# Second forward attention: wo products of kv heads 0 to 2 between the softmax steps of the last group

## The chip, the cores and the metric

The kernel runs on one core of a Trainium2 chip, in one launch. The metric is the time on the device in microseconds (us); the kernel before is given as the median of three runs.

## The reference

The program computes a small decode network and all its gradients. The forward pass is two layers, each an attention block A and a feed-forward block B, with the same weights in both:

```python
x = A_x                                        # (2, 1, 1024)
x = x + _A_ref(_layernorm(x), A_k_cache, A_v_cache, A_wq, A_wo)
x = x + _B_ref(_layernorm(x), B_w1, B_b1, B_w2, B_b2)
x = x + _A_ref(_layernorm(x), A_k_cache, A_v_cache, A_wq, A_wo)
x = x + _B_ref(_layernorm(x), B_w1, B_b1, B_w2, B_b2)
```

`_A_ref` makes 32 query heads of 128 from `x @ wq`, 8 for each of 4 kv heads, scores them against a K cache of 16384 rows for each batch and kv head, takes the softmax, multiplies with the V cache, and returns `o @ wo` with `wo` of 4096 x 1024. `_B_ref` normalises once more and is `gelu(y @ w1 + b1) @ w2 + b2` with F = 3584. The outputs are the result and the gradients for x, both caches, wq, wo, w1, b1, w2 and b2, from a given `grad_out`. Everything is bf16 outside the chip.

## The kernel before

**Stages.** The order in time is: attention forward of layer 0, feed-forward of layer 0, attention forward of layer 1, feed-forward of layer 1, then the backward passes in the reverse order, with the cache gradients of both layers written at the end. The program is written out in order by hand: each engine executes its instructions in the order in which the kernel issues them, and only semaphores stand between engines.

**Groups and steps.** A group is one of 8 pairs of batch and kv head (g = batch x 4 + kv head). `attn_fwd` (L561) walks over 8 groups x 4 chunks x 4 blocks = 128 slots, one per step: eight 128 x 128 blocks of K are transposed on PE (`emit_T`, L480), copied out of PSUM, and two steps later multiplied with q (`score`, L633). Other work is hung on later steps: `Sched.later(n, f)` runs `f` at the start of the step `n` further on, and `Sched.q` is a queue from which a step takes one entry after that (in every second step while there are slots, in each step afterwards). The walk goes on past the last slot until both are empty.

After a group's last score, `post` (L572) lays out its softmax: the maximum (`p1` and `p2`, 2 and 4 steps on), sixteen exponentials on ACT in pairs (`ex`, 5 to 12 steps on, the first eight for chunks 0 and 1), the products with V (`queue_acc`, four entries 9 steps on and four more, with the closing `fin`, 13 steps on), the sum of the exponentials (14 and 15 steps on). `fin` copies the accumulator out (`evac`, L516), and two steps later `reduce` (L524) folds it on PE and `finish` (L609) writes the group's column of `oT` on DVE. The accumulator is one PSUM tile `ACCT` of 128 x 512 (`acc_all` in the profile); even groups use its left half, odd groups the right.

**The wo product.** When the walk has ended, `attn_layer_fwd` (L805) copies `oT` into `o_all` (L817) and calls `w_fwd` (L341), which clears the left half of `ACCT` (L345) and goes over wo in 8 tiles of 512 rows, 1 MB each. `w_take` (L328, DMA at L331) takes a buffer and issues the load on SP's queue; `fwd_rows` (L334, matmul at L337) makes the 32 products of a tile, 128 x 128 weights against 128 x 32 columns, accumulating in PSUM. Tile k holds the rows of query heads 4k to 4k + 3, so tiles 0 to 5 belong to kv heads 0 to 2, and tiles 6 and 7 to kv head 3, whose second batch is the last group. Then `xA` (L820) adds the residual, two layer norms follow, and w1's 7 tiles and their products (`m_all`), `hpre` (L830), the gelu, and, since layer 1 is the last, the backward pass with w1's and wo's tiles (`weights_down`, L876).

**Buffers.** All streamed tiles (K, V and weights) share one pool `ld` of 7 buffers of 1 MB. A load on SP's queue waits until the last reader of its buffer is done, and whatever SP has to issue next waits behind it. The K and V tiles of group 7 (`keepK`, `keepV`) are loaded in layer 0 and stay in SBUF: `kv_load` (L464) issues nothing for them in layer 1.

Of the kernel before, what the change touches and what calls it, by code (L numbers as in the profile page):

```python
# [23 lines left out]
def kernel(  # L24
# [25 lines left out]
    V = nc.vector  # L50
# [3 lines left out]
    B, _, D = A_x.shape  # L54
    _, HKV, SK, DH = A_k_cache.shape
    assert B == 2 and DH == 128
    HQ = A_wq.shape[1] // DH
# [3 lines left out]
    DJ = D // 128  # L61
    FJ = F // 128
    HD = HQ * DH
    G = B * HKV
    T = SK // 128
    TC = 32
    NCH = T // TC
# [8 lines left out]
    WIDE = 32  # L76
# [56 lines left out]
    ACCT = pa([128, 512], F32, "acc_all")  # L133
# [177 lines left out]
    def w_tiles(W, n_in, n_out):  # L311

        out = []
        if n_out == 1024:
            for j0 in range(0, n_in // 128, 4):
                out.append((j0, 4, 0, 1024))
        elif n_out < 4096:
            for c0 in range(0, n_out, 1024):
                cw = min(1024, n_out - c0)
                nj = 4096 // cw  # L320
                for j0 in range(0, n_in // 128, nj):
                    out.append((j0, nj, c0, cw))
        else:
            for j0 in range(n_in // 128):
                out.append((j0, 1, 0, n_out))
        return out

    def w_take(W, j0, nj, c0, cw):  # L328
        wt = ld.tile([128, LDW], BF16, name="wt", tag="ld")
        wv = wt[:].rearrange("p (j n) -> p j n", j=nj)  # L330
        nc.sync.dma_start(wv, W[j0 * 128:(j0 + nj) * 128, c0:c0 + cw].rearrange("(j p) n -> p j n", p=128))  # L331
        return wv
# [8 lines left out]
    def w_fwd(W, n_in, n_out, x, between=None):  # L341
        JO = n_out // 128
        nw = min(WIDE, 512 // JO)
        fps = ACCT[:, 0:JO * nw].rearrange("p (j b) -> p j b", b=nw)
        V.memset(fps, 0.0)  # L345
        for j0, nj, c0, cw in w_tiles(W, n_in, n_out):
            fwd_rows(fps, nw, w_take(W, j0, nj, c0, cw), x, j0, c0 // 128)
            if between:
                between.popleft()()
        while between:  # L350
            between.popleft()()
        return fps[:, :, 0:2]
# [111 lines left out]
    def kv_load(w, g, c):  # L464
        keep = w + str(c) if g == G - 1 else w if (g, c) == (XG, 0) else None
        t = held_tiles[keep] if keep else ld.tile([128, LDW], BF16, name="kv_" + w, tag="ld")
        if keep not in held:
            src = Kv if w == "K" else Vv
            nc.sync.dma_start(t[:].rearrange("p (t d) -> p t d", d=128), src[g, :, c * TC:(c + 1) * TC, :])
            if keep:  # L470
                held.add(keep)
        return t[:].rearrange("p (t d) -> p t d", d=128)
# [85 lines left out]
                sc_.later(2, a.reduce)  # L558
            sc_.q.append(fin)

    def attn_fwd(l, q_bf, rbc, oT, groups):  # L561
        sch = Sched()
        slots = [(g, c, b) for g in groups for c in range(NCH) for b in range(NB)]
        kTs, sc, st = {}, {}, {}

        def max_half(g, f):
            m = small.tile([128, 8], F32, name="mx%d" % f)
            V.tensor_reduce(out=m[:], in_=sc[g][f][:], axis=AX.X, op=ALU.max)
            charge("D", 0.7)
            st[g].append(m)  # L570

        def post(g):  # L572
            max_half(g, 1)
            m0, m1 = st[g]
            V.tensor_tensor(out=m0[:], in0=m0[:], in1=m1[:], op=ALU.max)
            esum = small.tile([128, 2, 8], F32, name="esum")
            negm = small.tile([128, 8], F32, name="negm")
            box = {}

            def p1():  # L580
                box["pm"] = pm_([8, 128], F32, "pm")
                PE.transpose(box["pm"][:, :], m0[:], identf[:])
                gm = small.tile([8, 1], F32, name="gm")
                V.reduce_max(out=gm[:], in_=box["pm"][:, :], axis=AX.X)
                box["dg"] = small.tile([8, 8], F32, name="dg")
                V.tensor_scalar(out=box["dg"][:], in0=identf[0:8, 0:8], scalar1=gm[:, 0:1], scalar2=None, op0=ALU.mult)
                charge("D", 0.5)

            def p2():
                pm2 = pm_([128, 8], F32, "pm2")  # L590
                PE.matmul(pm2[:], lhsT=onesf[0:8, :], rhs=box["dg"][:], start=True, stop=True)
                V.tensor_scalar(out=negm[:], in0=pm2[:], scalar1=-1.0, scalar2=None, op0=ALU.mult)  # L592
                charge("D", 0.2)

            def ex(f, h):
                half = NP // 2
                S.activation(out=e_all[:, g, f * half:(f + 1) * half, l, h, :],  # L597
                             in_=sc[g][f][:, h, :].rearrange("p (a b) -> p a b", b=2),
                             func=ACT.Exp, bias=negm[:, h:h + 1], scale=1.0, accum_out=esum[:, f, h:h + 1])
                charge("A", 0.3)  # L600

            def fin1():
                V.tensor_tensor(out=esum[:, 0, :], in0=esum[:, 0, :], in1=esum[:, 1, :], op=ALU.add)

            def fin2():
                pm3 = part_sum(esum[:, 0, :], 8, "pm3")
                V.reciprocal(out=rbc[:, g, :], in_=pm3[:])

            def finish(ps):  # L609
                V.tensor_tensor(out=oT[:, g, :], in0=ps, in1=rbc[:, g, :], op=ALU.mult)  # L610

            a = Acc(g, "V", lambda u: e_all[:, g, u, l].rearrange("p h t -> p (h t)"), finish, g % 2)
            sch.later(2, p1)
            sch.later(4, p2)
            for i in range(16):
                sch.later(5 + i // 2, lambda i=i: ex(i // 8, i % 8))
            sch.later(9, lambda: queue_acc(sch, a, range(0, 2), False))
            sch.later(13, lambda: queue_acc(sch, a, range(2, 4), True))
            sch.later(14, fin1)
            sch.later(15, fin2)  # L620

        def score(s):
            g, c, b = slots[s]
            if c == 0 and b == 0:
                sc[g] = {}
                st[g] = []
            kT = kTs.pop(s)
            for j in range(8):
                t = c * TC + b * 8 + j
                f = t // TH  # L630
                if t % TH == 0:
                    sc[g][f] = px([128, 8, TH], F32, "sc")
                PE.matmul(sc[g][f][:, :, t % TH], lhsT=kT[:, j, :], rhs=q_bf[:, g, :], start=True, stop=True)  # L633
            if c == NCH // 2 - 1 and b == NB - 1:
                max_half(g, 0)
            if c == NCH - 1 and b == NB - 1:
                post(g)

        cv = None
        s = 0  # L640
        while s < len(slots) + 2 or sch.busy():
            sch.s = s
            if s < len(slots):
                g, c, b = slots[s]
                if b == 0:
                    cv = kv_load("K", g, c)
                kTs[s] = emit_T(cv, b, True)
            sch.run_slot(1 if s < len(slots) else 2)
            if 2 <= s < len(slots) + 2:
                score(s - 2)  # L650
            s += 1
# [138 lines left out]
    o_all = cols4(HQ, "o_all")  # L790
# [9 lines left out]
    ALLG = list(range(G))  # L800

    def lsl(l):
        return slice(2 * l, 2 * l + 2)

    def attn_layer_fwd(l, xT, between=None):  # L805
        y, rstd = ln_fwd(xT[:], f"a{l}")
        V.tensor_copy(out=n_all[:, 0:DJ, lsl(l)], in_=y[:])
        qps = w_fwd(A_wq, D, HD, n_all[:, 0:DJ, lsl(l)], between)
        qT_bf = vec.tile([128, G, 8], BF16, name=f"qT_bf{l}")
        for b in range(2):  # L810
            V.tensor_scalar(out=qT_bf[:, b * HKV:(b + 1) * HKV, :].rearrange("p k r -> p (k r)"), in0=qps[:, :, b],
                            scalar1=QSCALE, scalar2=None, op0=ALU.mult)
        rbc = vec.tile([128, G, 8], F32, name=f"rbc{l}")
        oT = vec.tile([128, G, 8], F32, name=f"oT{l}")
        attn_fwd(l, qT_bf, rbc, oT, ALLG)
        for b in range(2):
            V.tensor_copy(out=o_all[:, 0:HQ, 2 * l + b], in_=oT[:, b * HKV:(b + 1) * HKV, :].rearrange("p k r -> p (k r)"))  # L817
        aps = w_fwd(A_wo, HD, D, o_all[:, 0:HQ, lsl(l)])
        xn = vec.tile([128, DJ, 2], F32, name=f"xA{l}")
        V.tensor_tensor(out=xn[:], in0=aps, in1=xT[:], op=ALU.add)  # L820
        saved[f"a{l}"] = dict(y=y, rstd=rstd, qT_bf=qT_bf, rbc=rbc, oT=oT)
        return xn
# [559 lines left out]
    sch = Sched()  # L1382
# [128 lines left out]
    while 2 * m < NS + 2:  # L1511
# [7 lines left out]
        for k in range(2):  # L1519
            s = 2 * m + k  # L1520
            if s < NS:
                i, b = NCH + s // NB, s % NB
# [97 lines left out]
```

## Time and profile before

| what | value |
|---|---|
| three runs | 1137.77, 1140.46, 1141.27 us |
| median | 1140.46 us |
| the profiled execution: its own time | 1139.88 us |
| its span | 1138.1 us |
| mean granted PE clock | 0.857 of full speed |
| busy share of the span: PE, DVE, ACT, POOL | 80%, 54%, 47%, 6% |
| DMA, mean over the span | 395 GB/s, 449.2 MB |

The span is the profiled execution from its first to its last instruction, and all places in the text, such as "at 418 us", are measured from the span's start. Busy shares are averages over stages with different limits, so a stage is read in its own window. PE is the matmul engine and PEld its weight loads, DVE the vector engine, ACT the scalar engine, POOL the general one, and SP only issues DMAs. L-numbers are lines of the kernel before.

### The profile page before, as it was taken

How to read it: one execution, taken by the hardware profiler on the slowest of the kernel's cores; microseconds unless marked ns; L12 is line 12 of the kernel's file. 1: busy time of each engine (PE TensorE's matmuls, PEld its weight loads, DVE VectorE, ACT ScalarE, POOL GpSimd, SP SyncE). 2: the span in 40 equal slices, each digit the busy share in tenths (PEclk: the TensorE clock that was granted, in tenths of full speed). 3: DMA queues.
4: the chain of work that ended last, by engine and by line, in shares of the span. 5: the costliest groups of instructions: out<-in, count | busy, mean ns of one | idle time of the engine just before them, and what ended most of it. 6: DMA issues, size and time to landing. Idle time of an engine off the chain costs nothing.

```text
span 1138.1 us, 38123 instructions
## 1 busy us (share of the span) xinstructions
PE 915.9 (80%) x16766; PEld 674.7 (59%) x16767; DVE 619.8 (54%) x1363; ACT 534.0 (47%) x1356; POOL 70.2 (6%) x124
## 2 busy tenths in 40 slices
PE   4979795468888975789887678888898897899996
PEld 3867674358766754778765567755545454455552
DVE  1545451180545523654442246678798767786876
ACT  0544351005544420434333214468697766676764
POOL 0000000000000000000000000022121111111210
PEclk9988895567999875899998678999999978897978
DMA  8999999999999979999999699998999999999997
GB/s 371 423 425 425 424 424 413 395 413 423 423 425 423 412 288 404 388 422 421 399 413 393 232 380 309 370 386 302 403 419 421 421 419 424 423 411 421 423 385 290
DMA packets 104183, 449.20 MB, mean 395 GB/s; under 512 B 7238, under 2 KB 11334, under 8 KB 66896
## 3 DMA queue, kind: packets, MB, share of 16 engines
q1 hardware_dynamic: 86672, 354.46, 77.6%
q0 software_dynamic: 17344, 92.29, 19.6%
q8 instruction: 131, 2.15, 0.7%
q14 instruction: 36, 0.29, 0.1%
HBM read 348.14 MB, written 98.58 MB: 393 GB/s over the span
## 4 chain that ended last, share of the span: by engine, by line
PE 45%; DMA 35%; DVE 10%; issue 5%; ACT 4%; POOL 0%; SPq 0%; DVEq 0%; ACTq 0%; POOLq 0%
DMA kv_V<-in_A_v_cache_dram 13%; PE tp L480 10%; DMA wt<-in_B_w_dram 5%; PE acc_all L512 4%; PE tpm L1527 4%; DMA kv_K<-in_A_k_cache_dram 4%; PE xm L1336 4%; DMA wt<-in_A_wo_dram 3%; DMA out_dram<-keepK 3%; DMA keepK<-in_A_v_cache_dram 3%; PE sc L633 3%; PE xm L1250 2%; PE wtp L358 2%; PE dp L1389 2%; PE dp L726 2%
## 5 line engine op out<-in xcount | busy, mean ns | idle before, releaser
L159 ACT COPY kT<-tp 128x512 int32<-128x512 int32 x200 | 117.4, 587 | 298.4 <-PE tp L480 289.1
L162 DVE COPY kT<-tp 128x1024 bf16<-128x1024 bf16 x168 | 114.9, 690 | 141.8 <-PE tp L480 130.4
L480 PE MATMUL tp<-ident,kv_K 128*128 128x128 bf16 x1728 | 142.0, 230 | 6.9 <-DMA kv_K<-in_A_k_cache_dram 6.8
L480 PEld LDWEIGHTS <-kv_K 128*128 128x128 bf16 x1728 | 107.8, 103 | 7.7 <-DMA kv_K<-in_A_k_cache_dram 7.5
L170 DVE CAST big<-xm 128x512 bf16<-128x512 f32 x133 | 86.3, 684 | 19.3 <-PE xm L1336 14.3
L167 ACT CAST big<-xm 128x512 bf16<-128x512 f32 x151 | 82.1, 595 | 25.0 <-PE xm L1336 14.8
L633 PE MATMUL sc<-qT_bf,kT 128*128 128x8 bf16 x2048 | 91.5, 171 | 0.1
L633 PEld LDWEIGHTS <-kT 128*128 128x128 bf16 x2048 | 75.7, 97 | 26.7 <-issue 20.8
L337 PEld LDWEIGHTS <-wt 128*128 128x128 bf16 x1920 | 57.4, 104 | 54.7 <-issue 17.8
L167 ACT CAST keepV<-xm 128x512 bf16<-128x512 f32 (+1 forms) x137 | 75.0, 594 | 29.5 <-PE xm L1336 18.5
L480 PE MATMUL tp<-ident,kv_V 128*128 128x128 bf16 x864 | 70.2, 227 | 14.1 <-DMA kv_V<-in_A_v_cache_dram 12.2
L597 ACT ACTIVATE e_all<-sc,negm 128x64 bf16<-128x64 f32 x256 | 77.2, 343 | 1.0 <-DVE negm L592 1.0
L170 DVE CAST keepV<-xm 128x512 bf16<-128x512 f32 (+1 forms) x101 | 65.9, 684 | 18.9 <-PE xm L1336 12.7
L269 DVE STREAM_TRANSPOSE wt<-wt 128x512 int32<-128x512 int32 x104 | 63.6, 674 | 14.2 <-PE w2b_f L337 11.0
L512 PE MATMUL acc_all<-kv_V,e_all 128*16 128x256 bf16 x864 | 46.0, 293 | 28.7 <-DMA kv_V<-in_A_v_cache_dram 14.4
L159 ACT COPY wt<-wtp 128x512 int32<-128x512 int32 x72 | 40.3, 587 | 57.0 <-PE wtp L358 54.1
L480 PEld LDWEIGHTS <-kv_V 128*128 128x128 bf16 x864 | 55.2, 101 | 16.2 <-DMA kv_V<-in_A_v_cache_dram 13.1
L597 ACT ACTIVATION_READ_ACCUMULATOR e_all<-sc,negm 128x1 f32 x256 | 59.8, 234 | 0.0
L167 ACT CAST keepK<-xm 128x512 bf16<-128x512 f32 x98 | 53.0, 596 | 14.1 <-PE xm L1336 7.5
L1389 PE MATMUL dp<-wdo,kT 128*128 128x64 bf16 x896 | 52.8, 206 | 0.0
L358 PE MATMUL wtp<-ident,wt 128*128 128x128 bf16 x576 | 47.8, 244 | 4.9 <-ACT wt L159 2.6
L1336 PE MATMUL xm<-QmK,blk 64*128 64x512 bf16 x256 | 48.8, 444 | 2.3 <-ACT keepV L167 1.0
(387 smaller groups left out, 1564.4 us busy)
## 6 DMA issues: line engine op xcount, KB each, us to landing
kv_K<-in_A_k_cache_dram SPq DMA_DIRECT2D x81, 1024.0 KB, 13.0
kv_V<-in_A_v_cache_dram SPq DMA_DIRECT2D x81, 1024.0 KB, 12.9
wt<-in_B_w_dram SPq DMA_DIRECT2D x42, 1024.0 KB, 12.9
wt<-in_A_wo_dram SPq DMA_DIRECT2D x32, 1024.0 KB, 9.6
out_dram<-big POOLq DMA_DIRECT2D x26, 1024.0 KB, 18.9
out_dram<-keepV POOLq DMA_DIRECT2D x19, 1024.0 KB, 20.7
out_dram<-keepK POOLq DMA_DIRECT2D x17, 1024.0 KB, 17.8
wt<-in_A_wq_dram SPq DMA_DIRECT2D x16, 1024.0 KB, 11.0
```

Of the source, the lines that this page charges most:

```text
L159: S.copy(out=dst.bitcast(I32), in_=src.bitcast(I32))
L162: V.tensor_copy(out=dst, in_=src)
L167: S.copy(out=dst, in_=src)
L170: V.tensor_copy(out=dst, in_=src)
L269: V.transpose(out=w, in_=w)
L358: PE.transpose(tp[:, o, :], view[:, o * 128:(o + 1) * 128], ident[:])
L480: PE.transpose(tp[:, j, :], cv[:, b * 8 + j, :], ident[:])
L512: PE.matmul(self.acc[cg:cg + 16, :], lhsT=coef(u), rhs=self.cv[:, t:t + 2, :].rearrange("p t d -> p (t d)"), start=False, stop=True, tile_ ...
L597: S.activation(out=e_all[:, g, f * half:(f + 1) * half, l, h, :], in_=sc[g][f][:, h, :].rearrange("p (a b) -> p a b", b=2), func=ACT.Exp, ...
L633: PE.matmul(sc[g][f][:, :, t % TH], lhsT=kT[:, j, :], rhs=q_bf[:, g, :], start=True, stop=True)
L1336: PE.matmul(pss[k][:], lhsT=blk[p:p + 64, o + 2 * h + k // 2, :], rhs=Qm[p:p + 64, :, :].rearrange("p a b -> p (a b)"), start=True, stop=T ...
L1389: PE.matmul(dp[:, :, t:t + 4], lhsT=kT[:, j, :], rhs=wd[:, :, x:x + 4], start=(b + j == 0), stop=False)
```

## The change

In layer 1 the products of wo's tiles 0 to 5 are issued inside the walk of `attn_fwd`, after group 6 has finished; tiles 6 and 7 follow after it, as before. For that the left half of `ACCT` is cleared, and the part of `o_all` for kv heads 0 to 2 copied, one step after group 6's `finish`; the products of the six tiles are hung 2, 3, 8, 13, 15 and 15 steps after it. The copy for kv head 3 comes after the walk. In layer 0 all eight tiles come after the walk, with the clear ahead of the copy. `w_fwd` is no longer called for wo.

```diff
-    def attn_fwd(l, q_bf, rbc, oT, groups):
+    def attn_fwd(l, q_bf, rbc, oT, groups, early=None):
...
             def finish(ps):
                 V.tensor_tensor(out=oT[:, g, :], in0=ps, in1=rbc[:, g, :], op=ALU.mult)
+                if early and g == groups[-2]:
+                    for at, f in zip((1, 2, 3, 8, 13, 15, 15), early):
+                        sch.later(at, f)
...
-        attn_fwd(l, qT_bf, rbc, oT, ALLG)
-        for b in range(2):
-            V.tensor_copy(out=o_all[:, 0:HQ, 2 * l + b], in_=oT[:, b * HKV:(b + 1) * HKV, :].rearrange("p k r -> p (k r)"))
-        aps = w_fwd(A_wo, HD, D, o_all[:, 0:HQ, lsl(l)])
+        tiles = w_tiles(A_wo, HD, D)
+        heads = HQ // HKV * (HKV - 1)
+        n_early = heads // 4 if l == 1 else 0
+        x = o_all[:, 0:HQ, lsl(l)]
+        fps = ACCT[:, 0:DJ * WIDE].rearrange("p (j b) -> p j b", b=WIDE)
+        wv = {}
+
+        def o_in(k0, k1):
+            n = HQ // HKV
+            for b in range(2):
+                V.tensor_copy(out=o_all[:, k0 * n:k1 * n, 2 * l + b],
+                              in_=oT[:, b * HKV + k0:b * HKV + k1, :].rearrange("p k r -> p (k r)"))
+
+        def take(k):
+            wv[k] = w_take(A_wo, *tiles[k])
+
+        def open_early():
+            V.memset(fps, 0.0)
+            o_in(0, HKV - 1)
+            for c in range(NCH):
+                kv_load("V", G - 1, c)
+            for k in range(n_early):
+                take(k)
+
+        def rows(k):
+            fwd_rows(fps, WIDE, wv.pop(k), x, 4 * k, 0)
+
+        attn_fwd(l, qT_bf, rbc, oT, ALLG, [open_early] + [lambda k=k: rows(k) for k in range(n_early)] if n_early else None)
+        if not n_early:
+            V.memset(fps, 0.0)
+        o_in(HKV - 1 if n_early else 0, HKV)
+        for k in range(n_early, len(tiles)):
+            take(k)
+            rows(k)
+        aps = fps[:, :, 0:2]
```

## The prediction

> **What bounds the kernel now.** I read the page first, for the 40 slices. One slice is 28.45 us, so slice 15 is 398 to 427 us. The third line is what all DMA queues moved.
>
> ```profile
> DMA  8999999999999979999999699998999999999997
> GB/s 371 423 425 425 424 424 413 395 413 423 423 425 423 412 288 404 388 422 421 399 413 393 232 380 309 370 386 302 403 419 421 421 419 424 423 411 421 423 385 290
> ```
>
> The kernel lives on DMA: most slices stand at 410 to 425 GB/s. Slice 15, the end of the second forward attention, is the first deep hole, at 288. The windows around it place it: us, busy time and count of PE, PEld, DVE, ACT, POOL, then the granted clock, the DMA share and GB/s.
>
> ```profile
> 414.00:420.00 6.00, 4.58 (x77) 3.30 (x78) 1.48 (x7) 0.02 (x1) 0.00 (x0) 0.50 0.24 91
> 420.00:424.00 4.00, 4.00 (x157) 4.00 (x154) 0.00 (x0) 0.00 (x0) 0.00 (x0) 0.51 0.68 182
> 424.00:445.00 21.00, 10.16 (x274) 9.25 (x269) 3.53 (x17) 0.00 (x0) 2.11 (x5) 0.58 1.06 403
> ```
>
> From 414 to 424 the queue moved 6 x 91 + 4 x 182 = 1274 KB where 403 GB/s would have moved 4030: 2756 KB short, or 6.8 us of transfer time. Who holds it back is in the waits of SP's queue between 408 and 424 us (total, times, longest):
>
> ```profile
> SPq L331 <- PE acc_all L337: 13.7, 5, 11.3
> ```
>
> SP stood 11.3 us in one wait of `w_take` for a wo product: the load of wo's eighth tile needs the buffer of the first, of seven, and the first is read only after the last group's softmax. Last the chain of waits, 408 to 448 us (start, length), for what the hole costs:
>
> ```profile
> 409.18 4.86 ACT e_all L597 x32
> 414.03 0.04 issue
> 414.08 1.03 PE acc_all L512 x12
> ...
> 416.65 0.43 DVE acc_sb L170
> ...
> 418.96 1.03 PE acc_all L337 x32
> 420.00 0.02 issue
> 420.01 6.93 DMA wt<-in_A_wo_dram
> 426.95 0.04 issue
> 426.99 1.02 PE acc_all L337 x32
> ...
> 431.58 13.38 DMA wt<-in_B_w_dram
> ...
> 447.89 15.19 DMA wt<-in_B_w_dram
> ```
>
> Exponentials, value products, the copy of the accumulator and (left out) the reduction, the first wo products; then 6.93 us waiting for a tile that could only be asked for at 420.01; and from there two waits on w1 tiles (forward, landing 444.96; backward, landing 463.08). The DMA stream is unbroken from about 424 to 478 us, so these landings move with the moment at which the stream restarts.
>
> **What moves.** In the built program the order on SP, ACT and POOL is unchanged: six of wo's loads stood ahead on SP anyway, and the extra call for the last group's V tiles issues nothing, since those tiles stay in SBUF from the first layer. The matmuls are the same; wo groups of 32 stand elsewhere. Counting steps: the last group's `post` runs in step 129, group 6 finishes in 134, so the clear and the copy stand in 135, groups 0 and 1 in 136 and 137 (ahead of all value products, which begin in 138), group 2 in 142 (ahead of the second half), group 3 in 147 (behind the accumulator copy, ahead of the reduction), groups 4 and 5 in 149, behind it. Prices are in PE's order of time (start, length):
>
> ```profile
> 411.71 1.88 PE L512 MATMUL acc_all<-keepV,e_all 128*16 128x256 bf16 x32 [1.82 <-ACT e_all L597]
> 418.96 5.39 PE L337 MATMUL acc_all<-o_all,wt 128*128 128x32 bf16 x197 [0.82 <-DVE acc_all L345]
> ```
>
> 5.39 / 197 x 32 = 0.88 us for a group of 32. Five w1 groups, from 436.36, took 4.41 there, 0.88 each too.
>
> **Costs, step by step.** (1) DVE: group 6's `oT` stands at 409.93 in DVE's order of time. From `oT` to the first product, through two copies and the clear, took 418.19 to 418.96 = 0.77 us, so group 0 starts at 410.70. DVE idles there (3.96 us until L603), so this costs nothing; without that cover it would be 0.6 us. (2) Groups 0 and 1 run 410.70 to 412.46. Queued behind them on PE are the first half's 32 value products, ready at 411.71: they run 412.46 to 414.34 instead of ending at 413.59; the wait for the exponentials until 414.08 hides all but 0.26. (3) Group 2 runs to 415.22, and the second half, which took 414.08 to 416.65, ends at 417.79: 1.14 late. (4) The copy takes 0.48 to 418.27. Group 3 waits for it in this program, and the reduction waits behind group 3: 419.15, then 1.06 to `oT` at 420.21, against 418.19: the softmax tail is 2.0 us longer. (5) Groups 4 and 5 fill 420.2 to 421.9, over the last `oT` and copy (0.4 us, hidden; without that cover 0.4 on the path). Groups 6 and 7 end at 423.7, so `xA` comes at 423.7 instead of 428.04: 4.3 us sooner, because of eight groups (7.0 us) only two follow alone and the 6.93 us wait is gone.
>
> (6) SP: the eighth tile is asked for at 411.6, w1's first at 412.5, further ones at 415.2, 419.1, 421.0, 421.9, 422.8, 423.7. The seventh wo tile was issued at 408.3 and took:
>
> ```profile
> DMA to landing us min/median/max: 9.4/9.4/9.4
> ```
>
> so it lands at 417.7. Landings 426.95 to 444.96 are seven tiles in 18.01 us, 2.573 each. Behind 417.7 the next eight tiles, all asked for at least 6.93 us (the time from an idle queue) ahead of their turn, land at 420.3, ..., 438.3. The last w1 tile therefore lands 444.96 - 438.3 = 6.7 us sooner. (7) Is that what comes last? `xA` to the first w1 product took 8.32 us, so w1 products run 432.0 to 438.2 without waits; the last tile lands at 438.3. Both paths meet, DMA last by 0.1: `hpre` is 6.7 us sooner. (8) The first backward w1 tile needs the first w1 group's buffer, free at 432.9; 6.93 later is 439.8, and its turn is 440.9: the stream holds with 1.1 us to spare. The wait that ended at 463.08 ends 6.7 sooner as well, and all later stages start from there. The first layer gets the clear ahead of the copies, the same three DVE instructions in a row: nothing.
>
> Sum: -6.7 us on the profiled execution (span 1138.1 to 1131.4; its own time 1139.88 to 1133.2, which is 0.6 under the median), so 1140.46 becomes 1133.8.
>
> **Two rules weighed.** The row: the granted clock stood at 0.50 from 408 to 420 us and rose after PE had been full from 420 to 424. The Trainium skill, "TensorE: Matmul & The Clock Gate", Part 1, says that about 3.4 us of sustained work releases the half-rate clock. By that rule the change, which keeps PE nearly full from 410.7, would release it near 415 us, an estimate, and PE's part after that would be shorter; the sum would stay, since DMA is last.
>
> The row: 6.93 us from an idle queue to landing. The Trainium skill, "DMA: Bandwidth & Descriptors", Anatomy of one DMA, fits 2.0 us plus bytes over 436e3 (for another issue path), 4.4 us for these tiles; by it the spare time in (8) would be 3.6 us, and the sum the same.
>
> **Rivals.** A, PE's order eats the head start: groups 0 to 3 stand ahead of products on the critical chain, and if they cost it 6 us instead of 2, `xA` stays at 428.04. Then the first backward w1 load is still issued at 437.39 and lands at 444.3, where the stream could have had it at 440.9: a 3.4 us hole comes back and 447.48 - 444.3 = 3.2 us is left: 1137.3. For it: the landings of wo's first four tiles are not in the trace, and group 0 blocks PE until its tile is there. Against: 2.573 us apart back from 417.7, the first landed near 402, the third near 407.
>
> B, the lead is spent downstream: from 464 to 480 us the chain runs on PE and DVE, and SP's longest wait there is 9.3 us for a wo product of the backward pass. If that stage did not start earlier, the time is the old one, 1140.5. Against: in the chain it starts from the landing at 463.08.
>
> C, slower: the clock of the last stage. Between 720 and 1080 us PE is busy 317 us at granted clocks of 0.77 to 1.00 by stretch, 0.903 on average. If the shifted work is granted less, PE's time there grows in proportion: at 0.884 (2.1% less) the gain is gone, at 0.874 (10.1 us lost) the kernel is over 0.3% slower, at 0.865 it is 13.9 - 6.7 = 7.2 us slower, 1147.7. For it: the clock does wander between stretches. Against: the three runs lie within 3.5 us.
>
> That the change does nothing is excluded by the order on PE: 64, 32 and 32 products stand between the steps.
>
> **How the numbers follow.** Forecast 0.75, A 0.12, B 0.08, C 0.05. A measurement tells about 0.3% (3.4 us, 1137.04) from no change; A lies at that border, so half of it counts as faster: faster 0.81, same 0.06 + 0.08 = 0.14, slower 0.05. Low end: the whole hole of 6.8 us and a run as far below the median as the fastest shown (2.7): 1130.9. High end: A with the slowest run's 0.8 above the median: 1138.1. B and C and part of A's spread stay outside.
>
> **What would show it.** Right: 403 GB/s or so through 414 to 424 us; no SP wait of 11 us on a wo product; wo groups on PE from about 410.7; `oT` of the last group near 420.2, later than before; `xA` near 423.7; w1's wait ending near 438.3; every later stage about 6.7 us sooner. Wrong: a DMA hole of over 2 us anywhere between 410 and 445; PE waiting at 410.7 for a wo tile; `xA` after 426; or the lead shrinking between 464 and 500.

## The result and the profile after

The changed kernel takes 1133.13 us (median of 7 runs, 1131.23 to 1135.79) against 1140.46 us (7 runs, 1137.06 to 1143.24): ratio 0.9938, 95% interval 0.9922 to 0.9955, so 5.1 to 8.9 us faster. The profiled execution took 1133.13 us, its span is 1131.4 us.

The page's slices first. A slice is now 28.28 us long, and slice 15 is 396 to 424 us. It moved 382 GB/s where the kernel before moved 288:

```profile
DMA  8999999999999999999999699997999999999997
GB/s 371 424 424 424 424 424 414 398 415 423 422 425 419 402 382 402 390 420 419 391 408 394 239 371 350 374 382 284 401 397 421 423 419 424 423 387 418 423 423 308
```

The windows of the same places (busy time of PE, PEld, DVE, ACT, POOL, granted clock, DMA share, GB/s):

```profile
414.00:420.00 6.00, 4.73 (x121) 3.25 (x114) 0.80 (x3) 1.15 (x8) 0.00 (x0) 0.78 1.05 404
420.00:424.00 4.00, 3.56 (x106) 3.46 (x103) 0.38 (x3) 0.00 (x0) 0.00 (x0) 0.50 1.05 401
424.00:445.00 21.00, 9.82 (x277) 9.31 (x274) 7.26 (x35) 0.25 (x1) 2.11 (x5) 0.50 1.05 400
```

91 and 182 GB/s have become 404 and 401: the hole is gone, and none of its size follows up to 445 us. SP's longest wait for a wo product between 408 and 424 us, 11.3 us before, is 3.5:

```profile
SPq L331 <- PE acc_all L337: 10.9, 6, 3.5
```

And the chain of waits, 405 to 460 us (start, length; L337 is a wo or w1 product, L512 a value product; "issue" is time in which the engine waits for nothing that the profile names):

```profile
411.73 1.87 PE acc_all L337 x64
413.59 1.81 PE acc_all L512 x31
415.40 0.93 PE acc_all L337 x32
416.33 0.43 PE acc_all L512 x11
416.76 0.74 issue
417.50 0.39 PE acc_all L512 x5
417.89 0.32 PE pm L189 x2
418.21 0.57 PE acc_all L512 x16
418.80 0.44 DVE acc_sb L170
419.24 0.04 issue
419.28 1.02 PE acc_all L337 x32
420.30 0.84 PE o_ps L527 x4
...
422.99 0.44 issue
...
433.55 5.19 PE acc_all L337 x189
438.74 0.64 issue
439.37 1.12 PE acc_all L337 x35
...
441.72 16.35 DMA wt<-in_B_w_dram
```

The wo groups stand where the order put them, and the 6.93 us wait for a wo tile has left the chain. So has the wait for the forward w1 tiles, 13.38 us long before: their products now run behind the layer norms, 433.55 to 440.49, with one stop of 0.64 us that is no wait for a tile: it stands three products before the last tile's. The backward w1 wait remains; it ends at 458.07 instead of 463.08.

### The profile page after: what moved, and what is told of

Its sections match the earlier page's. It is cut to its first block, busy times and chain, and to the rows that moved or that the text cites. A ratio compares the mean times of both kernels' runs of the same rounds, so it can differ in the third digit from the quotient of the medians.

```text
span 1131.4 us, 38126 instructions
## 1 busy us (share of the span) xinstructions
PE 919.7 (81%) x16767; PEld 678.4 (60%) x16767; DVE 620.1 (55%) x1365; ACT 533.1 (47%) x1356; POOL 70.1 (6%) x124
## 4 chain that ended last, share of the span: by engine, by line
PE 45%; DMA 38%; DVE 10%; issue 4%; ACT 3%; POOL 0%; SPq 0%; DVEq 0%; POOLq 0%; ACTq 0%
DMA kv_V<-in_A_v_cache_dram 15%; PE tp L480 9%; DMA wt<-in_B_w_dram 4%; PE acc_all L512 4%; PE tpm L1561 4%; DMA kv_K<-in_A_k_cache_dram 4%; PE xm L1370 3%; DMA keepK<-in_A_v_cache_dram 3%; DMA wt<-in_A_wo_dram 3%; PE xm L1284 3%; DMA out_dram<-keepV 3%; PE sc L636 3%; PE wtp L358 2%; PE dp L1423 2%; PE dp L729 2%
## 5 line engine op out<-in xcount | busy, mean ns | idle before, releaser
L480 PE MATMUL tp<-ident,kv_K 128*128 128x128 bf16 x1728 | 146.8, 235 | 5.3 <-DMA kv_K<-in_A_k_cache_dram 5.3
L480 PEld LDWEIGHTS <-kv_K 128*128 128x128 bf16 x1728 | 111.3, 105 | 6.0 <-DMA kv_K<-in_A_k_cache_dram 5.9
L337 PEld LDWEIGHTS <-wt 128*128 128x128 bf16 x1920 | 57.4, 104 | 50.4 <-issue 18.7
L512 PE MATMUL acc_all<-kv_V,e_all 128*16 128x256 bf16 x864 | 46.1, 293 | 28.0 <-DMA kv_V<-in_A_v_cache_dram 15.1
L170 DVE CAST keepK<-xm 128x512 bf16<-128x512 f32 x69 | 44.8, 683 | 7.4 <-PE xm L1370 5.2
```

What stands on the lines that cost most here:

```text
L170: V.tensor_copy(out=dst, in_=src)
L337: PE.matmul(fps[:, o0 + o, :].rearrange("p (a b) -> p a b", b=2), lhsT=wv[:, j, o * 128:(o + 1) * 128], rhs=x[:, j0 + j, :].unsqueeze(1).t ...
L480: PE.transpose(tp[:, j, :], cv[:, b * 8 + j, :], ident[:])
L512: PE.matmul(self.acc[cg:cg + 16, :], lhsT=coef(u), rhs=self.cv[:, t:t + 2, :].rearrange("p t d -> p (t d)"), start=False, stop=True, tile_ ...
```

## The experiments

Two theories, and a rival from the prediction. **S**: the gain is the DMA stream that no longer stops, worth what is filled of the 6.8 us hole. **P**: the gain is what PE no longer has to do behind the softmax, worth what `xA` comes sooner. **A**: PE's order is critical, so a longer softmax tail is paid for. C, in the first expectations, is the gain coming from clock or order alone. All differences are against the kernel before, run beside each experiment (35 and 28 runs), each experiment 7 to 12 runs. Single profiled executions reach the tail at slightly different times (group 6's `oT` between 408.8 and 411.1 us), so places compared between two of them carry an error of one to two us.

**1. Loads free, products late.**

```diff
-        aps = w_fwd(A_wo, HD, D, o_all[:, 0:HQ, lsl(l)])
...
+            wv = [w_take(A_wo, *t) for t in w_tiles(A_wo, HD, D)]
+            for k in range(8):
+                fwd_rows(fps, WIDE, wv[max(k, 6)], o_all[:, 0:HQ, lsl(l)], 4 * k, 0)
```

> The kernel before, with one edit in layer 1: all eight groups of wo products stay behind the last softmax, but groups 0 to 5 multiply the weights of tile 6 instead of their own (so the wo product is not the reference's), and the buffers of wo's first five or six tiles are free as soon as their loads have landed. Loads run ahead, no product moves. Theory S (the gain is the DMA stream of w1 that no longer stops): the stream is unbroken, the last forward w1 tile lands near 438.3 instead of 444.96; PE has its eight groups in a row, 418.96 to 426.0, so xA near 426.0 and hpre near 440.5: 5.5 us faster than before (5 to 6.7). Theory P (the gain is what the change takes from PE behind the softmax, that is how much sooner xA comes): xA 2.0 us sooner, so 2.0 us faster. A theory by which the gain came from PE's order or its clock gives nothing here: 0.

Measured: ratio 0.9960 (0.9940 to 0.9979), 4.6 us faster with not one product moved. P's 2.0 lies outside the interval (2.4 to 6.8), S's 5.5 inside. `xA` came at 427.48, 0.6 sooner than before; the 2.0 of the expectation lost 1.54 us to a stop of PE among the wo products that the chain puts to "issue" (see the last section). What S had too high stands in the later windows:

```profile
424.00:434.00 10.00, 4.25 (x77) 3.72 (x74) 2.37 (x14) 0.00 (x0) 0.97 (x2) 0.66 1.05 402
434.00:445.00 11.00, 6.12 (x224) 6.12 (x224) 3.63 (x15) 0.25 (x1) 1.13 (x4) 0.50 0.87 314
```

The first hole is filled and a second opens, 314 GB/s: with `xA` late, the first w1 products are late, their buffer comes free late, and the first backward w1 load is issued at 436.8 instead of the change's 434.6. This is rival A's mechanism (a hole behind a late `xA`), seen where no product was moved. Moving the products closes this second hole.

**2. Products early, the whole stream held.**

```diff
+        def hold():
+            V.tensor_copy(out=lock[:, 1, :], in_=lock[:, 0, :])
+            nc.sync.dma_start(lock[:, 0, :], A_x.rearrange("b s d -> (b s) d")[:, 0:16])
...
         for k in range(n_early, len(tiles)):
+            if l == 1 and k == len(tiles) - 1:
+                hold()
             take(k)
             rows(k)
```

> The changed kernel, with one edit: the load of wo's eighth tile, and so all that stands behind it on SP, waits until DVE has done the last group's copy into o_all (a 32-element load behind a small DVE copy is put ahead of it). Products stay where the change put them, the stream restarts when it did before. Theory S: the eighth tile is asked for near 420.8 instead of 420.0, so the time is that of the kernel before, 0 to 1 us slower; the hole of 6 to 7 us in DMA is back. A theory by which taking four groups of products (3.5 us) off PE behind the softmax, less the 2 us longer tail, is worth something by itself: 1.5 to 3.3 us faster. Theory C (the clock, or the order on PE): the gain of the change stays, 5 to 7 us.

Measured: ratio 0.9995 (0.9975 to 1.0015): no gain. The wait of SP's queue and the windows of this run:

```profile
SPq L851 <- DVE lock L850: 11.1, 1, 11.1
```

```profile
414.00:420.00 6.00, 4.21 (x126) 3.69 (x124) 1.07 (x6) 0.00 (x0) 0.00 (x0) 0.92 0.24 89
420.00:424.00 4.00, 1.03 (x39) 0.92 (x35) 0.00 (x0) 0.00 (x0) 0.00 (x0) 0.50 0.84 273
```

With all six groups where the change puts them and PE with little left to do from 420 on (1.03 of 4 us busy, 4.00 before), the 11 us wait and the 89 GB/s are back, and so is the time. The early products alone buy nothing that can be measured, and C's 5 to 7 us fall. P does not fall by this run: its 1.5 to 3.3 lies in part inside the interval (1.7 slower to 2.8 faster).

**3. The same hold, one load later.** `hold()` stands behind `take` of the eighth tile instead of ahead of it, so that only w1's loads wait.

> The changed kernel, with the same hold one load later: wo's eighth tile is asked for early as in the change, w1's tiles wait for the last group's copy. xA is as early as in the change. Theory S: w1's first tile is asked for near 420.8 and lands near 427.7, the seventh at 427.7 + 6 x 2.573 = 443.1 instead of 444.96: 1.9 us faster than before. Theory P: xA 4.3 us sooner, so 4.3 us faster. Theory C: 5 to 7 us faster.

Measured: ratio 0.9982 (0.9962 to 1.0001), 2.1 us faster; S said 1.9, P 4.3, the edge of the interval (0.1 slower to 4.3 faster). `xA` came at 424.26, 3.8 us sooner than before, and `hpre` only 1.4 sooner: it waited for w1. One tile more moved early than in experiment 2, and the time is 1.5 us better:

```profile
414.00:420.00 6.00, 4.67 (x123) 3.31 (x111) 0.80 (x3) 0.83 (x6) 0.00 (x0) 0.78 0.81 309
420.00:424.00 4.00, 4.00 (x132) 4.00 (x131) 0.43 (x4) 0.00 (x0) 0.00 (x0) 0.65 0.25 45
```

**4 and 5. Two early tiles, one early tile.**

```diff
-        n_early = heads // 4 if l == 1 else 0
+        n_early = 2 if l == 1 else 0
```

> The changed kernel with only two of wo's tiles early (the products of tiles 0 and 1, at the places the change gives them); tiles 2 to 7 behind the last softmax. Two buffers come free early, which keep DMA busy for 5.1 us; the third comes free near 419.9, so w1's second tile lands near 426.8 where its turn was 425.4. Theory S: 1.4 us of the 6.7 are lost, 5.3 us faster than before. Theory P: the tail is 0.26 us longer instead of 2.0 and six groups follow it, xA near 424.3, 3.7 us faster.

> The changed kernel with only wo's tile 0 early; tiles 1 to 7 behind the last softmax. Theory S: one buffer comes free early, 2.57 us of the hole are filled; the next is free near 419.8 and its load lands near 426.8, where the unbroken stream has w1's first tile at 422.8: 4.0 us are lost, 2.7 us faster than before (two tiles gave 5.7, six 7.3). Theory P (xA): the tail is not longer, seven groups follow it without the wait of 6.93 us, xA near 425.1: 2.9 us faster. The two agree here; the run is for the dose: if the gain of the two-tile version came from its first tile, or from PE's order, one tile gives 5 to 6 as well.

Measured: two tiles 0.9950 (0.9929 to 0.9971), 5.7 us; one tile 0.9968 (0.9948 to 0.9989), 3.6 us; six gave 7.1 by their ratio. The order is S's (5.3, 2.7 and 6.7), but P's too (3.7, 2.9 and 4.3), and the intervals of one and two overlap, so these two runs tell little apart by themselves; the steps between them rest on the amounts of DMA below more than on the times.

**6. All six groups in one row, ahead of the value products.**

```diff
-                    for at, f in zip((1, 2, 3, 8, 13, 15, 15), early):
+                    for at, f in zip((1, 2, 3, 3, 3, 3, 3), early):
```

> The changed kernel with all six early groups in one row, ahead of all value products of the last group (3, 3, 3 and 3 steps after group 6's finish instead of 8, 13, 15, 15). Group 5's tile lands near 415.4, so the value products start 2 to 3 us later than in the change and the last softmax's end (oT) is near 422.5 instead of 420.2, the tail 4 us longer than before. Theory S: the buffers come free at 411.6 to 416.5, ahead of every turn, the stream is unbroken; xA near 424.5; the last w1 tile near 438.3: 6 to 7 us faster than before, the same as the change. Rival A (PE's order is critical): the 2 us longer tail comes out of the gain, 4 to 5 us faster.

Measured: ratio 0.9954 (0.9937 to 0.9971), 5.2 us (3.3 to 7.2). From group 6's `oT` to the last group's was 12.78 us, against 8.26 before: the tail is 4.5 us longer. The interval holds both S's 6 to 7 and A's 4 to 5, so the time does not tell them apart. The amounts are in between: DMA moved 390 GB/s from 414 to 445, 11 less than the change. PE's order of time shows why:

```profile
417.67 1.57 PE L337 MATMUL acc_all<-o_all,wt 128*128 128x32 bf16 x53 [2.18 <-issue]
```

PE stopped 2.18 us in the middle of the fifth group, whose tile had landed at 412.9, with no wait that the profile names (see the last section).

**7. Early products in layer 0 as well.**

```diff
-        n_early = heads // 4 if l == 1 else 0
+        n_early = heads // 4
```

> The changed kernel with the early products in both layers. In layer 0 the wo tiles land from 187.8 to 205.8 at 2.57 us apart in a stream without a hole (397 to 428 GB/s in every 4 us from 160 to 216), and products wait for each landing. With the edit the first group stands ahead of the last softmax's value products and waits for the landing at 187.8: oT of the last group comes near 199 instead of 187.9. Theory S: no hole, so nothing to gain, and nothing is lost, because the last landing at 205.8 still sets xA: layer 0's xA within 0.5 us of 206.9, the time that of the change, 6 to 8 us faster than before. Rival A (a longer tail costs what it is long): layer 0 is 11 us later, the kernel 3 to 5 us slower than before. A theory by which moved products are worth something by themselves: another 3 to 6 us faster than the change.

Measured: ratio 0.9945 (0.9926 to 0.9964), 6.3 us: the gain of the change, no more and no less. PE's order of time in layer 0 (start, length):

```profile
187.89 1.03 PE L337 MATMUL acc_all<-o_all,wt 128*128 128x32 bf16 x32 [9.17 <-DMA wt<-in_A_wo_dram]
190.45 1.04 PE L337 MATMUL acc_all<-o_all,wt 128*128 128x32 bf16 x32 [1.52 <-DMA wt<-in_A_wo_dram]
191.42 1.88 PE L512 MATMUL acc_all<-keepV,e_all 128*16 128x256 bf16 x32
...
205.85 1.03 PE L337 MATMUL acc_all<-o_all,wt 128*128 128x32 bf16 x32 [1.55 <-DMA wt<-in_A_wo_dram]
```

PE stood 9.17 us in front of the first wo tile with the value products queued behind; the last group's `oT` came at 198.06 instead of 187.90. `xA` came at 206.92 instead of 206.87, because the last wo landing sets it in both. The same move of the same products, without a hole in DMA: a softmax tail 10 us longer and no effect on the time.

**8. The groups fitted into PE's gaps.**

```diff
-                    for at, f in zip((1, 2, 3, 8, 13, 15, 15), early):
+                    for at, f in zip((1, 2, 3, 12, 15, 15, 15), early):
```

> A version meant to be better than the change: groups 0 and 1 as in the change, group 2 placed behind all value products ahead of the accumulator's copy (so that PE works while DVE copies, 12 steps after group 6's finish), groups 3 to 5 behind the reduction. The tail is 0.7 us longer than before instead of 2.0, buffers come free at 411.6, 412.5, 418.1, 420.0, 420.9, 421.8, and only the third is at the edge of its turn (418.5). Theory S: same stream, the last w1 tile near 438.3; xA near 423.2, 0.5 us sooner than in the change: 7 us faster than before, 0 to 0.5 us faster than the change, which five rounds hardly tell apart. Rival A: 1.3 us faster than the change.

Measured: ratio 0.9949 (0.9924 to 0.9974), 5.8 us. The tail is 0.5 us longer than before (8.78 us), as meant, but the version does not beat the change in the measurement: the intervals cover each other.

**All runs together.** The third column is the mean GB/s from 414 to 445 us in one profiled execution. Each missing GB/s of 403 is 31/403 = 0.077 us of transfer; the kernel before lacks 89, or 6.8 us. The fourth column is how much of that a run has filled. The last is how much sooner `xA` came, counted in each execution from its own group 6's `oT` (18.1 us in the kernel before), because the executions reach that point at different times.

| kernel | faster by, us (95%) | GB/s | of the hole filled, us | `xA` sooner after `oT`, us |
|---|---|---|---|---|
| the change | 7.1 (5.1 to 8.9) | 401 | 6.7 | 4.0 |
| 1, loads free | 4.6 (2.4 to 6.8) | 372 | 4.5 | 0.5 |
| 2, stream held | 0.6 (-1.7 to 2.8) | 326 | 0.9 | 0.7 |
| 3, w1 held | 2.1 (-0.1 to 4.3) | 338 | 1.8 | 4.6 |
| 4, two early | 5.7 (3.3 to 8.1) | 393 | 6.1 | 3.2 |
| 5, one early | 3.6 (1.3 to 5.9) | 368 | 4.2 | 3.5 |
| 6, in one row | 5.2 (3.3 to 7.2) | 390 | 5.8 | 3.0 |
| 7, both layers | 6.3 (4.1 to 8.4) | 396 | 6.3 | 4.0 |
| 8, in the gaps | 5.8 (3.0 to 8.7) | 395 | 6.2 | 3.9 |

The time follows the fourth column within 0.6 us in every row; with intervals of about 2 us to either side, so close an agreement is in part luck. It doesn't follow the last: experiment 3 brought `xA` sooner than the change did and gained a third of what it gained, experiment 5 brought it nearly as much sooner and gained half, and experiment 1 hardly moved `xA` and gained 4.6. Against P speak above all the change and experiment 1, where the last column lies 1.1 and 1.9 us below the interval of the gain; in 3, 4, 6 and 7 it lies outside by 0.1 to 0.3 us only, and in 2, 5 and 8 inside.

## Why the prediction was right

**The hole and its owner.** 2756 KB short, 6.8 us: filled in the change to 401 GB/s. That SP's wait for the first wo buffer makes it is shown from both sides: freeing the buffers without moving products fills it (experiment 1), holding the loads with the products moved brings it back (2, 3).

**Steps (1) to (5), PE.** Predicted for the softmax tail: 2.0 us longer. Between the two `oT` of DVE's order it is 10.12 against 8.26 us, 1.9 longer. Groups 0 and 1 took 1.87 us (1.76 in the sum), and the other groups stood at their places. That the total fits is in part luck: two things that the sum did not have cancel. The second half of the value products, with the sum of the exponentials, held PE for 1.73 us instead of 2.57, at a granted clock that had risen by then (below), and in its middle PE stopped for 0.74 us. `xA` was put at 423.7 and came at 425.22; 1.1 of that is that this execution reached group 6's `oT` at 411.06 instead of 409.93, and 0.4 is a stop of PE (0.44 us, "issue") among the last groups that the sum did not have.

**Step (6), the landings.** The eighth tile landed at 420.6 (predicted 420.3), the last forward w1 tile at 438.8 (438.3). The seventh wo tile itself landed 0.4 later than in the execution before, so the spacing was right.

**Step (7), which path is last.** The two were said to meet within 0.1 us, DMA last. With `xA` 1.5 later, PE was last instead: the last w1 tile lay ready at 438.8 and `hpre` came at 440.52 instead of the 439.4 that the steps give, 5.6 us sooner than before instead of 6.7. The sum's term for PE was too short here: besides the late `xA`, PE stopped for 0.64 us at 438.74, which no term had. Of the 1.5 us by which `xA` was late, 1.1 are this execution's late start. The backward w1 wait ended 5.0 sooner (463.08 to 458.07), not 6.7: the last forward tile landed 0.5 late, and from there the seven backward tiles took 19.3 us instead of 18.1. DMA moved 403 GB/s in both of these stretches, so why they took longer stays open.

**Step (8), the margin.** The first backward w1 load was issued at 434.6, where the steps said 432.9, and landed at 441.5, 6.9 later and 2.7 behind the forward one: the stream held, but the predicted 1.1 us to spare were used up. Experiment 1 shows what lies beyond the margin: issued at 436.8, landed at 442.1, and 314 GB/s. From issue to landing it took 5.3 us there and 6.3 in experiment 6 (435.4 to 441.8), so the 6.93 us, with which the margin and rival A were worked out, are no fixed price.

**The rivals.** A has a real mechanism but a smaller price: the tail grew as much as predicted, and the 10 us that experiment 7 added to layer 0's cost nothing that can be measured (experiment 6, with 4.5 us in layer 1, doesn't decide it). B did not come: the lead is 5.5 us at the copy behind the backward w1 products (468.75 to 463.24) and still 5.0 at 494.85 us (489.84 in the change). It is 6.7 us at the end of the span, but "every later stage about 6.7 us sooner" did not hold, and that the span is 1131.4 to the tenth is luck: between these places the lead of this one execution, taken from the starts of the same instructions on DVE, wanders from under 1 to over 7 us. Before 400 us, where both programs do the same, it already wanders by about 2 us either way, and the measured gain itself is known to 2 us only. C did not come: between 720 and 1080 us the mean granted clock was 0.877, below the 0.884 that should have cost the whole gain, and the gain stayed. PE's busy time there is 321 us instead of 317, where the price assumed 327. The price put on the clock was too high; no run here isolates why.

**The clock rule.** The granted clock was 0.53 from 412 to 416 us and 0.89 from 416 to 420, against 0.50 in both before. That agrees with the release near 415 us that the prediction worked out by the rule in the Trainium skill, "TensorE: Matmul & The Clock Gate", Part 1. The clock was back at 0.50 from 420 to 424, though PE was busy for 2.73 of the 4 us before and 3.56 of these 4.

## What to carry to other kernels

Where loads are prefetched into a ring of buffers, as here, the first consumer's place in the program decides when the stream goes on, so look for the point at which the DMA rate falls and ask which reader holds the next buffer. Move just enough of these readers ahead of the long chain: the first two of six tiles brought most of the gain here. In layer 0 (experiment 7) the delay that they put on the chain cost nothing, because the stream, not the chain, ended last, and it bought nothing, because the stream had never stopped.

## What was not expected of the hardware

PE stops inside a row of ready products for 0.4 to 2.2 us, with no wait that the profile names: 1.12 us before (at 424.4), 0.74, 0.44 and 0.64 us in the change, 1.54 us in experiment 1, 2.18 us in experiment 6. They are as large as the differences between the versions of the order tried here, and were in no sum.

Their times change with the order, but not their place in PE's instructions, counted over all that the trace records of it: weight loads, products and 35 of its sequencer. The stops of the kernel before and of experiment 1 come at the same instruction as the 0.44 us of the change; that of experiment 6 comes 256 instructions earlier, at that of the change's 0.74 us. In all ten traces, all 142 such stops of over 0.3 us lie a multiple of 256 instructions apart (to within one), and each ends 1.2 to 1.6 us after a packet of DMA queue 8, of the kind "instruction" (packets, MB, share of 16 engines):

```profile
q8 instruction: 131, 2.15, 0.7%
```

Its 131 packets of 16.4 KB are as many as the 33,568 instructions recorded of PE in the kernel before make full blocks of 256. So PE most likely waits at these places for its next block of instructions. A dense row uses one up fast: 128 weight loads with their 128 products take 3.5 us, an estimate from the 0.88 us for 32. No run here moved the boundaries of the blocks, which would be the test.
